# Pooled attention and a SoLU MLP on one core: x's lower half in two steps, the first product by banks, spreading matrices by ScalarE, a new order

## The chip, the core and the metric

The kernel runs on one core of one Trainium2 chip. The core has five engines that each work through their own instructions in order: TensorE (PE, matrix products), VectorE (DVE), ScalarE (ACT), GpSimd (POOL) and SyncE (SP), which here issues all DMAs. An engine that has to wait for another holds up everything that stands behind on its own line. TensorE works from SBUF into PSUM; PSUM's banks hold 512 float32 columns for 128 partitions each. The metric is device time in microseconds, the median of several executions.

## The reference, cut to what matters

```python
# q, k, v: (8 batches, 8 heads, 576 rows, 64)
k_p = k.reshape(B, H, Sp, pool, D).mean(axis=3)      # pool 8: 72 rows
v_p = v.reshape(B, H, Sp, pool, D).mean(axis=3)
scores = scale * np.matmul(q, k_p.transpose(0, 1, 3, 2))
attn = softmax(scores)                               # over 72
x = np.matmul(attn, v_p)                             # -> 4608 tokens x 512
h = x @ w_in                                         # 512 -> 1024
solu = h * softmax(h)                                # over 1024
ln = (solu - mean) / sqrt(var + 1e-6) * g_ln
out = ln @ w_out                                     # 1024 -> 512
```

q, k and v are float32; w_in, w_out and g_ln come as 64-bit floats, which the kernel reads as words and converts itself.

## The kernel before

**Precision.** Each number that goes into a product is split into an upper half in float16 and a lower half, the rest, also in float16. Each product is then three products of halves: upper with upper, upper with the weight's lower half, lower with upper.

**Tiles.** The 4608 tokens are 36 tiles of 128. Every pair of batches has nine: four tiles of the first batch, one mixed tile (64 tokens of each batch), four of the second. Tile 4 is the first mixed one.

**One tile's way.** Its queries are split (`q_hi`, `q_lo`) and transposed by a DMA (qT); TensorE makes the scores; VectorE takes their maximum, the difference, the sum and the division, ScalarE the exponential; the shares e are split (`e_hi` on ScalarE, `e_lo` on GpSimd) and transposed by a DMA (eT, L848). TensorE multiplies them with the pooled V (`av`, L865) into a PSUM tile hp of two banks, of which there are two. Out of hp ScalarE makes x's upper half (`x_hi`, L873) and VectorE the lower (`x_lo`, L879), both for all 512 columns (bank 0 holds the chunks c = 0, 1 of x, bank 1 the chunks 2, 3). The first product (`mm1`, L897, 24 matmuls) then writes hp over with the 1024 columns of h, 512 in each bank. VectorE takes the maximum (`h_max`, L907), ScalarE the exponential (`h_exp`), VectorE the product with it and its sum (`z_mul`, L942); ScalarE centres it and makes the upper half, GpSimd the lower (`z_lo`), each is transposed by a DMA (zT, L972), and TensorE makes the second product (`mm2`, L1029, 24 matmuls in one bank). ScalarE evicts it (`o_evac`, L1037) and a DMA stores it (L1047 for a mixed tile, L1050 for the others).

**The first product's order.** It has three parts of eight matmuls. EARLY is 1: for every tile but the first, parts 0 and 1 take the upper half of x, two of the four chunks each, with both halves of the weight; part 2 takes x's lower half. Within each the two banks take turns (`for f in range(2)`). The whole product waits for both halves of x.

**Pooled V.** GpSimd adds the rows of V in groups of 8 (L346, three halvings) and VectorE takes the largest of them (`amx_v`, L366). TensorE carries the maximum over the partitions (gv, L375), and from it VectorE makes a scale in four steps, the last into `sv` (L388 to L400). Part of the pooled V has then to lie in other partitions, which TensorE does by a product with matrices of zeros and ones: `pick`, filled by 24 casts of VectorE before anything else (L255), is read by `v_ex` (L482), and `v_put` (L488) writes the result, vbr, on VectorE.

**What sets the order.** The function records 2,255 operations in a list, each with an engine, what it reads and writes and a due time, and then calls them in the order of a table of numbers, ORDER. The order of the calls is each engine's order; the engines' waits for each other follow from the tiles that the calls read and write. A buffer of a pool that is asked for again waits for the readers of the one before.

Of the kernel before, what the change touches and what calls it, by code (L numbers as in the profile page):

```python
# [12 lines left out]
AF = mybir.ActivationFunctionType  # L13
# [5 lines left out]
S14 = float(2**14)  # L19
# [148 lines left out]
def kernel(  # L168
# [10 lines left out]
    nc = tc.nc  # L179
    B, H, S, D = q.shape  # L180
# [8 lines left out]
    R1 = SP - R0  # L189
# [1260 lines left out]
```

## Time and profile before

| | us |
|---|---|
| median of 3 runs | 491.08 (490.11 to 492.01) |
| profiled execution | 492.35 |
| its span | 490.6 |
| TensorE busy | 440.0 (90%) |
| VectorE busy | 358.8 (73%) |
| ScalarE busy | 351.5 (72%) |
| GpSimd busy | 322.0 (66%) |

The span is the time from the first to the last instruction that the profiler saw; the rest of the execution's time lies around it. A share of the whole span is a mean over stretches with different limits: in the first 60 us the weights are converted and the first tiles start, later the tiles follow each other at an even pace, so shares are to be read by stretch. The tables give a start in us from the span's start, a time in us, the engine, the line and the operation; "x16" are 16 instructions of one form in a row, and a bracket gives how long the engine had idled before and who ended it.

### The profile page before, as it was taken

The numbers are of one execution on the slowest core, as the hardware profiler recorded it, in microseconds if no ns is written. First come the engines' busy times: TensorE is split into PE (matmuls) and PEld (weight loads), VectorE is DVE, ScalarE is ACT, GpSimd is POOL, SyncE is SP. The second block draws the span as 40 slices with busy tenths as digits, with TensorE's granted clock in tenths as the row PEclk, the third lists the DMA queues.
The fourth block names the chain that finished last, engine by engine and source line by source line (L and its number), as shares of the span: only waits on it lengthen the run. The fifth ranks groups of instructions, "written<-read, shape, count | busy, mean of one in ns | idle before, by whom it ended". The sixth has DMA issues, their size and how long they took to land.

```text
span 490.6 us, 12671 instructions
## 1 busy us (share of the span) xinstructions
PE 440.0 (90%) x4890; PEld 213.3 (43%) x4890; DVE 358.8 (73%) x867; ACT 351.5 (72%) x584; POOL 322.0 (66%) x469
## 2 busy tenths in 40 slices
PE   0076779899997999999999999989999999999996
PEld 0033334354443444544444444444444544544463
DVE  6898999859876596778686876777668866847530
ACT  1796988868973679677878677758787877765671
POOL 4235499786886588794688768946679666453350
PEclk9998999999999899999999999999999999999999
DMA  8999896999799878999889987995996786752742
GB/s 287 353 231 293 199 171 138 210 202 178 192 197 215 178 122 182 218 183 175 229 195 205 209 139 180 208 190 125 202 215 163 185 164 126 133 125 53 154 108 64
DMA packets 198460, 89.51 MB, mean 182 GB/s; under 512 B 174208, under 2 KB 182656, under 8 KB 197888
## 3 DMA queue, kind: packets, MB, share of 16 engines
q1 hardware_dynamic: 198400, 88.70, 85.4%
q8 instruction: 38, 0.62, 0.5%
q14 instruction: 22, 0.18, 0.1%
HBM read 37.75 MB, written 9.44 MB: 96 GB/s over the span
## 4 chain that ended last, share of the span: by engine, by line
PE 49%; DMA 17%; POOL 12%; DVE 10%; ACT 6%; issue 3%; SPq 2%; POOLq 0%; DVEq 0%; ACTq 0%
PE op L1029 22%; PE hp L897 21%; DMA zT<-z 5%; DMA qr<-in_q_dram 5%; DMA vr<-in_v_dram 4%; POOL z L964 2%; PE hp L865 2%; PE sc L772 2%; DMA eT<-e 2%; POOL vr L346 2%; POOL kr L346 2%; DVE z L942 1%; ACT z L956 1%; POOL e L841 1%; DVE pick L255 1%
## 5 line engine op out<-in xcount | busy, mean ns | idle before, releaser
L1029 PE MATMUL op<-wo,zT 128*128 128x512 f16 (+1 forms) x888 | 199.5, 376 | 3.8 <-DMA zT<-z 2.9
L897 PE MATMUL hp<-wi,xT 128*128 128x512 f16 x864 | 195.2, 379 | 4.6 <-DVE xT L879 4.6
L897 PEld LDWEIGHTS <-xT 128*128 128x128 f16 x864 | 83.4, 98 | 103.5 <-issue 4.2
L1029 PEld LDWEIGHTS <-zT 128*128 128x128 f16 x888 | 84.2, 98 | 98.9 <-DMA zT<-z 5.7
L964 POOL TENSOR_TENSOR z<-z,z 128x512 f16<-128x512 f32 x71 | 82.3, 1170 | 53.8 <-ACT z L951 46.9
L907 DVE TENSOR_REDUCE m<-hp 128x1 f32<-128x1024 f32 x36 | 43.9, 1221 | 31.3 <-PE hp L897 31.1
L346 POOL TENSOR_TENSOR vr<-vr 128x256 f32<-128x256 f32 (+2 forms) x48 | 42.3, 883 | 23.8 <-DMA vr<-in_v_dram 23.1
L841 POOL TENSOR_TENSOR e<-e,e 128x512 f16<-128x512 f32 x36 | 42.0, 1168 | 20.6 <-ACT e L833 20.5
L956 ACT ACTIVATE z<-z,sz 128x1024 f16<-128x1024 f32 x36 | 41.2, 1145 | 19.6 <-DVE z L942 19.2
L942 DVE SCALAR_TENSOR_TENSOR z<-hp,rs,z 128x1024 f32<-128x1024 f32 x36 | 46.1, 1281 | 6.2 <-ACT z L918 4.9
L918 ACT ACTIVATE z<-hp,nb,Hb 128x1024 f32<-128x1024 f32 x32 | 38.3, 1198 | 14.1 <-DVE nb L910 13.5
L1037 ACT ACTIVATE osb<-op,f 128x512 f32<-128x512 f32 (+1 forms) x37 | 24.8, 669 | 30.4 <-issue 9.9
L346 POOL TENSOR_TENSOR kr<-kr 128x512 f32<-128x512 f32 (+3 forms) x48 | 40.8, 858 | 7.4 <-DMA kr<-in_k_dram 6.7
L951 ACT ACTIVATE z<-z,sz 128x1024 f32<-128x1024 f32 x36 | 41.2, 1145 | 0.9
L751 POOL TENSOR_TENSOR q<-qr,q 128x512 f16<-128x512 f32 x28 | 32.4, 1157 | 10.8 <-ACT q L741 10.7
L796 DVE TENSOR_REDUCE sc<-sc 128x8 f32<-128x576 f32 x36 | 27.4, 761 | 15.5 <-ACT sc L792 15.5
L977 ACT ACTIVATE junk<-z 128x1024 f16<-128x1024 f32 x36 | 37.7, 1048 | 0.3
L782 DVE TENSOR_REDUCE mx<-sc 128x8 f32<-128x576 f32 x36 | 27.0, 751 | 14.6 <-PE sc L772 13.6
L879 DVE SCALAR_TENSOR_TENSOR xT<-hp,xT 128x512 f16<-128x512 f32 x36 | 24.6, 683 | 14.0 <-ACT xT L873 13.7
L873 ACT ACTIVATE xT<-hp 128x512 f16<-128x512 f32 x36 | 21.3, 591 | 17.9 <-PE hp L865 17.8
L811 DVE TENSOR_TENSOR e<-sc,r 128x576 f32<-128x576 f32 x36 | 27.2, 756 | 2.2
L785 DVE TENSOR_TENSOR sc<-sc,mx 128x576 f32<-128x576 f32 x36 | 27.4, 762 | 0.8
(229 smaller groups left out, 584.3 us busy)
## 6 DMA issues: line engine op xcount, KB each, us to landing
qr<-in_q_dram SPq DMA_DIRECT2D x16, 512.0 KB, 5.2
kr<-in_k_dram SPq DMA_DIRECT2D x16, 512.0 KB, 5.0
out_dram<-osb SPq DMA_DIRECT2D x31, 256.0 KB, 3.0
wor<-in_moe_w_out_dram SPq DMA_DIRECT2D x4, 1024.0 KB, 11.3
vr<-in_v_dram SPq DMA_DIRECT2D x8, 512.0 KB, 4.5
vr<-in_v_dram SPq DMA_DIRECT2D x16, 256.0 KB, 6.0
wo<-in_moe_w_in_dram SPq DMA_DIRECT2D x2, 1024.0 KB
wir<-in_moe_w_in_dram SPq DMA_DIRECT2D x2, 1024.0 KB
```

The source lines that it names most:

```text
L346: nc.gpsimd.tensor_tensor(out=dst, in0=x[:, :, :n], in1=x[:, :, n : 2 * n], op=ALU.add)
L751: nc.gpsimd.tensor_tensor(out=q_dst(i, 1), in0=q_src(i), in1=q_dst(i, 0), op=ALU.subtract)
L841: nc.gpsimd.tensor_tensor(out=m[:, 1], in0=em, in1=m[:, 0], op=ALU.subtract)
L897: nc.tensor.matmul(hp[:, f], lhsT=xT[:, xt, 2 * (c % 2) + c // 2], rhs=wi[:, wt, c, f * 512 : (f + 1) * 512], start=(part == 0 and n == 0) ...
L907: nc.vector.tensor_reduce(out=small(i, "m"), in_=tl[i]["hp"], axis=AX.XY, op=ALU.max)
L918: nc.scalar.activation(z, t["hp"], AF.Exp, bias=t["nb"], scale=hsc(i, 0), accum_out=small(i, "se"))
L942: nc.vector.scalar_tensor_tensor(out=t["z"], in0=t["hp"], scalar=t["rs"], in1=t["z"], op0=ALU.mult, op1=ALU.mult, accum_out=small(i, "sz"),)
L951: nc.scalar.activation(t["zf"], t["zf"], AF.Identity, bias=t["sz"], scale=-float(DFF))
L956: nc.scalar.activation(t["z16"][:, 0], t["zf"], AF.Identity, bias=t["sz"], scale=-float(DFF))
L964: eng.tensor_tensor(out=t["z16"][:, 1, fs], in0=t["zf"][:, fs], in1=t["z16"][:, 0, fs], op=ALU.subtract)
L977: nc.scalar.activation(junk, t["zf"], AF.Square, scale=DFF**-0.5, accum_out=small(i, "V"))
L1029: nc.tensor.matmul(op_, lhsT=zT[:, zt, c], rhs=wo[:, wt, c, cols(hf)], start=(part == 0 and n == 0), stop=(part == 2 and n == len(todo) - 1),)
```

## The change

Four things. The 24 casts that fill `pick` are gone from VectorE; a new operation `spreader`, called four times, does it in four ScalarE copies each, and `v_ex` is recorded as a reader of `pick`. `x_lo` takes an index j and makes one bank's half (128x256). `mm1` goes by banks: part 0 all products of x's upper half into bank 0, part 1 those into bank 1, part 2 those of the lower half; part 0 is recorded behind the lower half's first step, part 1 behind its second. And ORDER is another table, 2,295 numbers, of which two lines stand for all.

```diff
 ORDER = (
-    3, 4, 177, 178, 12, 110, 0, 50, 2, 56, 179, 1, 180, 181, 51, 182, 183, 52, 185, 186, 231,
+    1, 3, 7, 181, 4, 54, 55, 8, 56, 2, 6, 60, 9, 10, 0, 182, 183, 184, 185, 186, 5, 11, 21, 25,
...
-    for j in range(2):
-        for n in range(HB):
-            c, g = divmod(n, 2)
-            unit = ident[:, 64 * j + 4 * c + 2 * j + g : 64 * j + 64 : H]
-            for x, s in ((0, 0), (1, 1), (0, 2)):
-                at = 64 * j + 32 * c + 8 * s
-                nc.vector.tensor_copy(out=pick[:, x, n, at : at + 8], in_=unit)
...
+    def spreader(n):
+        c, g = divmod(n, 2)
+        for x, ss in ((0, slice(0, 4, 2)), (1, slice(1, 2))):
+            for j in range(2):
+                to = pick[:, x, n, 64 * j + 32 * c : 64 * j + 32 * c + 32]
+                to = to.rearrange("p (s r) -> p s r", r=R1)[:, ss]
+                at = 64 * j + 4 * c + 2 * j + g
+                unit = ident[:, at : 64 * j + 64 : H]
+                nc.scalar.activation(to, unit.unsqueeze(1).to_broadcast(to.shape), AF.Copy)
...
-    def x_lo(i):
+    def x_lo(i, j):
         xT = tl[i]["xT"]
+        cs = slice(2 * j, 2 * j + 2)
         nc.vector.scalar_tensor_tensor(
-            out=xT[:, 1].rearrange("p (t c) m -> p t (c m)", t=2), in0=tl[i]["xp"],
-            scalar=1.0 / S14, in1=xT[:, 0].rearrange("p (t c) m -> p t (c m)", t=2),
+            out=xT[:, 1, cs].rearrange("p c m -> p (c m)"), in0=tl[i]["xp"][:, j],
+            scalar=1.0 / S14, in1=xT[:, 0, cs].rearrange("p c m -> p (c m)"),
             op0=ALU.mult, op1=ALU.subtract,
         )
...
             xt, wt = ((0, 0), (1, 0), (0, 1))[part]
-            todo = [(c, xt, wt) for c in range(CI)]
+            todo = [(f, c, xt, wt) for c in range(CI) for f in range(2)]
         elif part < 2:
-            todo = [(c, 0, wt) for c in (2 * part, 2 * part + 1) for wt in range(2)]
-        else:
-            todo = [(c, 1, 0) for c in range(CI)]
-        for n, (c, xt, wt) in enumerate(todo):
-            for f in range(2):
-                nc.tensor.matmul(
-                    hp[:, f], lhsT=xT[:, xt, 2 * (c % 2) + c // 2], rhs=wi[:, wt, c, f * 512 : (f + 1) * 512],
-                    start=(part == 0 and n == 0), stop=(part == 2 and n == len(todo) - 1),
-                )
+            todo = [(part, c, 0, wt) for c in range(CI) for wt in range(2)]
+        else:
+            todo = [(f, c, 1, 0) for c in range(CI) for f in range(2)]
+        for f, c, xt, wt in todo:
+            nc.tensor.matmul(
+                hp[:, f], lhsT=xT[:, xt, 2 * (c % 2) + c // 2],
+                rhs=wi[:, wt, c, f * 512 : (f + 1) * 512],
+                start=(c == 0 and xt == 0 and wt == 0), stop=(part == 2 and c == CI - 1),
+            )
...
-        op("pe", 0.28, t + 7.5, v_ex, b, r=[("vrt", b)], w=[("x", "v", b)])
+        op("pe", 0.28, t + 7.5, v_ex, b, r=[("vrt", b), ("pick",)], w=[("x", "v", b)])
...
-        op("dve", 0.69, t(-1, 8.2), x_lo, i, r=[("h", i)], w=K("xT1"), u=K("xT"), after=[n])
+        for j in range(2):
+            op("dve", 0.42, t(-1, 8.2 + 0.5 * j), x_lo, i, j, r=[("h", i)], w=[("xT1", i, j)],
+               u=K("xT"), after=[n])
...
-                ws = [(nm, "wi", d) for nm in ("whi", "wlo") for d in (2 * c, 2 * c + 1)]
+                ws = [(nm, "wi", d) for nm in ("whi", "wlo") for d in range(4)]
+                ws += [("xT1", i, c)]
             else:
-                ws = K("xT1")
-            prev = [op("pe", 1.727, t(0, 1.78 * c), mm1, i, c, r=K("xT", "xT1") + ws, w=[("h", i)],
+                ws = []
+            prev = [op("pe", 1.727, t(0, 1.78 * c), mm1, i, c, r=K("xT") + ws, w=[("h", i)],
                        after=prev if c else ready)]
```

**At the start, VectorE.** The first fence is VectorE's line before, from the maximum of the pooled V (`amx_v`) to the next tile's score maximum (mx); sc, r and e are softmax steps of tile 1, u_wo and wor the conversion of a chunk of w_out.

```order
L366 TENSOR_REDUCE amx_v<-vp_92 128x1
L796 TENSOR_REDUCE sc_369<-sc_369 128x2x4
L802 TENSOR_SCALAR sc_369<-sc_369 128x2x4
L806 RECIPROCAL r_445<-sc_369 128x8
L811 TENSOR_TENSOR e_447<-sc_369,r_445 128x576
L388 TENSOR_REDUCE pv_454<-gv_452 128x1
L393 TENSOR_SCALAR pv_454<-pv_454 128x1
L210 TENSOR_SCALAR pv_454<-pv_454 128x1
L400 RECIPROCAL sv_455<-pv_454 128x1
L533 TENSOR_SCALAR u_wo_437<-u_wo_437 128x1024
L554 SCALAR_TENSOR_TENSOR wor_354<-wor_354,u_wo_437 128x1024
L782 TENSOR_REDUCE mx_527<-sc_477 128x8
```

The same place in the new order:

```order
L362 TENSOR_REDUCE amx_v<-vp_92 128x1
L384 TENSOR_REDUCE pv_429<-gv_427 128x1
L389 TENSOR_SCALAR pv_429<-pv_429 128x1
L213 TENSOR_SCALAR pv_429<-pv_429 128x1
L396 RECIPROCAL sv_430<-pv_429 128x1
L802 TENSOR_REDUCE sc_360<-sc_360 128x2x4
L808 TENSOR_SCALAR sc_360<-sc_360 128x2x4
L539 TENSOR_SCALAR u_wo_438<-u_wo_438 128x1024
L812 RECIPROCAL r_446<-sc_360 128x8
L817 TENSOR_TENSOR e_452<-sc_360,r_446 128x576
L560 SCALAR_TENSOR_TENSOR wor_416<-wor_416,u_wo_438 128x1024
L788 TENSOR_REDUCE mx_513<-sc_464 128x8
```

The four steps to `sv` have moved from behind the softmax of tile 1 to directly behind `amx_v`.

**In tile 5, VectorE.** Before, x's lower half of tile 5 (xT5) stood between the maximum of tile 4's h (m4) and tile 7's score maximum (mx7); pz4, nb4 and rs4 are tile 4's small factors. Here the rows carry what each instruction waits for.

```order
L907 TENSOR_REDUCE m4_1576<-hp4_1453 128x1 [waits PE_49]
L910 TENSOR_SCALAR nb4_1579<-m4_1576,Hm0_1562 128x1 [waits DVE_49,Activation_49]
L879 SCALAR_TENSOR_TENSOR xT5_1619<-hp5_1586,xT5_1619 128x512 [waits Activation_49]
L782 TENSOR_REDUCE mx7_1673<-sc7_1624 128x8 [waits PE_49]
L925 TENSOR_SCALAR pz4_1675<-nb4_1579 128x1 [waits DVE_49]
```

In the new order, down to tile 4's `z_mul`:

```order
L914 TENSOR_REDUCE m4_1577<-hp4_1443 128x1 [waits PE_49]
L886 SCALAR_TENSOR_TENSOR xT5_1612<-hp5_1579,xT5_1612 128x256 [waits Activation_49]
L917 TENSOR_SCALAR nb4_1666<-m4_1577,Hm0_1515 128x1 [waits DVE_49]
L932 TENSOR_SCALAR pz4_1668<-nb4_1666 128x1 [waits DVE_49]
L937 TENSOR_SCALAR pz4_1668<-pz4_1668 128x1 [waits DVE_49]
L788 TENSOR_REDUCE mx7_1693<-sc7_1616 128x8 [waits PE_49]
L941 RECIPROCAL pz4_1668<-pz4_1668 128x1 [waits DVE_49]
L886 SCALAR_TENSOR_TENSOR xT5_1612<-hp5_1579,xT5_1612 128x256 [waits PE_49]
L943 TENSOR_SCALAR rs4_1699<-pz4_1668,Hm0_1515 128x1 [waits DVE_49]
L791 TENSOR_TENSOR sc7_1616<-sc7_1616,mx7_1693 128x2x288
L949 SCALAR_TENSOR_TENSOR z4_1670,sz4_1702<-hp4_1443,rs4_1699,z4_1670 128x1024 [waits DVE_49,Activation_49]
```

The one step on xT5 has become two with six others between them; the second half waits for TensorE, the first, like the whole before, for ScalarE.

**Ahead of tile 9's eT, SyncE.** Before, from the transpose qT10 to the transpose eT9; osb4 is the output of the mixed tile 4, zT7 the transposes of tile 7's z.

```order
L758 DMA_TRANSPOSE qT10_2226<-q16_10_2026 128x8x128
L301 DMA vr3_1_2231<-in_v_dram 64x2x512 x2
L758 DMA_TRANSPOSE qT11_2236<-q16_11_2087 128x8x128
L972 DMA_TRANSPOSE zT7_2249<-z16_7_2247 128x8x128
L1047 DMA out_0_dram<-osb4_2075 64x512 x2
L972 DMA_TRANSPOSE zT7_2249<-z16_7_2247 128x8x128
L307 DMA vr3_2_2317<-in_v_dram 64x1x512 x2
L1050 DMA out_0_dram<-osb6_2245 128x512
L316 DMA qr3_2410<-in_q_dram 128x4x256
L848 DMA_TRANSPOSE eT9_2428<-e16_1_101 128x10x128
```

In the new order, from the store of osb4 on:

```order
L1054 DMA out_0_dram<-osb4_2070 64x512 x2
L764 DMA_TRANSPOSE qT10_2160<-q16_10_2157 128x8x128
L764 DMA_TRANSPOSE qT11_2223<-q16_11_2037 128x8x128
L303 DMA vr3_2_2277<-in_v_dram 64x1x512 x2
L1057 DMA out_0_dram<-osb5_2311 128x512
L979 DMA_TRANSPOSE zT7_2408<-z16_7_2289 128x8x128 x2
L854 DMA_TRANSPOSE eT9_2469<-e16_1_101 128x10x128
L1057 DMA out_0_dram<-osb6_2155 128x512
```

The store of osb4 has moved from between the two transposes of z to ahead of qT10, and eT9 stands directly behind both of them, with the store of osb5 before them.

## Rows read from the trace of the kernel before

**Rows 1.** Busy us by stretch: PE, PEld, DVE, ACT, POOL; then clock, DMA, GB/s.

```profile
7.40:13.00 5.60, 0.37 (x2) 0.10 (x1) 5.60 (x26) 0.01 (x1) 4.31 (x5) 1.00 1.04 392
49.90:61.00 11.10, 9.31 (x118) 4.49 (x118) 10.97 (x25) 10.29 (x22) 5.16 (x9) 1.00 0.85 182
...
160.20:163.60 3.40, 3.40 (x31) 1.31 (x22) 2.14 (x4) 1.31 (x3) 0.19 (x1) 0.50 1.18 147
...
163.70:486.90 323.20, 317.85 (x3487) 155.78 (x3485) 225.40 (x552) 234.31 (x393) 215.00 (x315) 1.00 0.81 165
```

**Rows 2.** PE's waits (us, times, longest), 98 to 491; last line: 49 to 98.

```profile
PE hp L865 <- DMA eT<-e: 3.5, 3, 2.6
...
PE sc L772 <- DVE pq('b', 6)_5636 L393: 0.3, 1, 0.3
...
PE hp L897 <- DVE xT L879: 4.6, 3, 1.8
```

**Rows 3.** The chain of waits: start, us, what.

```profile
7.48 5.50 DVE pick L255 x24
...
23.76 11.65 DMA vr<-in_v_dram
...
37.69 0.46 POOL vp L346
...
49.90 3.61 PE hp L897 x16
...
54.02 1.85 PE hp L897 x8
...
55.90 1.23 DVE m L907
```

**Rows 4.** Duration by line: ns min/median/max, first and last start, forms.

```profile
L835 ACT ACTIVATE e<-e x72: 238/242/258, 33.5 to 452.3; 128x64 f16<-128x64 f32 x72
...
L879 DVE SCALAR_TENSOR_TENSOR xT<-hp,xT x36: 639/681/692, 49.2 to 461.6; 128x512 f16<-128x512 f32 x36
...
L746 DVE SCALAR_TENSOR_TENSOR q<-qr,sq('b', 0)_174,q x8: 472/500/1265, 14.7 to 37.0; 128x256 f16<-128x256 f32 x8
...
L897 PE MATMUL hp<-wi,xT x864: 376/379/390, 49.9 to 467.4; 128*128 128x512 f16 x173
```

**Rows 5.** VectorE's instructions in order of time, 39 to 50 us.

```profile
39.27 0.49 DVE L366 TENSOR_REDUCE amx_v<-vp 128x1 bf16<-128x320 f32 x1 [1.29 <-POOL vp L346]
39.67 0.76 DVE L796 TENSOR_REDUCE sc<-sc 128x8 f32<-128x576 f32 x1
...
41.59 0.28 DVE L388 TENSOR_REDUCE pv<-gv 128x1 f32<-128x128 f32 x1
...
42.36 0.68 DVE L533 TENSOR_SCALAR u_wo<-u_wo 128x1024 int32<-128x1024 int32 x1
...
45.05 0.74 DVE L782 TENSOR_REDUCE mx<-sc 128x8 f32<-128x576 f32 x1
...
47.17 0.42 DVE L488 CAST vbr<-vx 128x256 f16<-128x256 f32 x1 [0.78 <-PE vx L482]
...
48.11 0.76 DVE L785 TENSOR_TENSOR sc<-sc,mx 128x576 f32<-128x576 f32 x1
...
49.16 0.68 DVE L879 SCALAR_TENSOR_TENSOR xT<-hp,xT 128x512 f16<-128x512 f32 x1
```

**Rows 6.** TensorE's instructions in order of time, 150 to 164 us.

```profile
153.13 3.62 PE L1029 MATMUL op<-wo,zT 128*128 128x512 f16 x16
159.36 0.36 PE L865 MATMUL hp<-eT,vb 64*64 64x128 f16 x12 [2.61 <-DMA eT<-e]
...
160.41 3.48 PE L1029 MATMUL op<-wo,zT 128*128 128x512 f16 x8
```

**Rows 7.** SyncE's DMAs in order of time, 147 to 156 us.

```profile
147.45 1.22 SPq L1047 DMA_DIRECT2D out_dram<-osb  x2
```

**Rows 8.** ScalarE's instructions in order of time, 147 to 156 us.

```profile
151.58 0.69 ACT L1037 ACTIVATE osb<-op,f 128x512 f32<-128x512 f32 x1 [3.75 <-DMA out_dram<-osb]
```

More of the change, by code (lines that the diff above doesn't have):

```diff
@@ L1243 @@
     home_free = []
+    for n in range(HB):
+        op("act", 0.85, 0.5 + n, spreader, n, w=[("pick",)])
     loads_kv(0, "kr", 0.0, 0.01)
@@ L1332, in tile @@
                 ws = (
-                    [("whi", "wi", d) for d in range(4)], K("xT1"),
+                    [("whi", "wi", d) for d in range(4)] + [("xT1", i, j) for j in range(2)], [],
                     [("wlo", "wi", d) for d in range(4)],
```

277 rows, old and new, of the table ORDER are left out of this document.

## The prediction

> **What bounds the kernel now.** I read the busy times by stretch first. From 163.7 us to the end of the products TensorE is busy 317.85 of 323.20 us [rows 1]; VectorE works 225.40 of them, ScalarE 234.31, GpSimd 215.00. There a change pays only in what TensorE waits for or loses. Before that others set the pace: in 49.9 to 61.0 us VectorE is busy 10.97 of 11.10 us and TensorE 9.31. Next, who TensorE waits for after 98 us [rows 2]: five rows from 3.5 us (the transpose eT, one wait of it 2.6) down to 0.3, 3.5 + 1.9 + 1.7 + 0.7 + 0.3 = 8.1 us. Last the chain of waits at the start [rows 3]: 5.50 us of the 24 casts that write `pick`, then 11.65 us of V's load, and the first product starts only at 49.90 us.
>
> **The casts leave VectorE.** 5.5 us go from VectorE's line; the 16 small ScalarE copies that replace them are like the 128x64 copy of 0.242 us [rows 4], so 3.9 us. ScalarE is busy 0.01 of 5.60 us where the casts stood [rows 1], which hides them; if they stuck out, only the matmuls with `pick` near 47 us would wait for them, so zero. But the 5.5 us don't come out of the first product's start. What follows on the chain is V's load, and its DMAs stand on SyncE behind the same loads and the same two transposes as before, so I leave its landing at 35.41 us (23.76 + 11.65). GpSimd's three additions behind it end near 38.2 in the new order (the third starts at 37.69 and takes 0.46 [rows 3], with no e work between now), against `amx_v` at 39.27 before [rows 5]. In the new order the four steps that give `sv` follow on `amx_v` directly, without tile 1's softmax (39.67 to 41.59 before). So `sv` is there at 38.2 + 0.5 + 0.3 (a matmul and two hand-overs, 0.22, 0.03 and 0.06 as below) + 0.8 (41.59 to 42.36) = 39.8, not 42.4: 2.6 earlier. Behind it now stand, ahead of `vbr`: softmax 1.9, shift and tail of w_out 2.7 (42.36 to 45.05), the maximum 0.7 and the difference 0.8 = 6.1, so `vbr` at 45.9 to 46.0, not 47.17. From there to the lower half of x 2.0 us before, 2.2 now (the quarter maximum of q comes behind `vbr`), and two halves take 0.16 longer than the whole. The first product moves from 49.90 to about 49.1: -0.8. Bounds: +0.5, if V's load lands later by the load of g that now stands in front of its second part, and -5.5, if the whole of the casts came off the front.
>
> **x's lower half in two steps.** One whole takes 681 ns [rows 4]. A half isn't in the trace. From 512 to 1024 columns out of PSUM VectorE's time grows to 1.23 us (the maximum [rows 3]), by 0.55, which takes a half to 0.41 us; the nearest 256-column one, out of SBUF, took at least 472 ns. I take 0.42, between them: 0.16 us more per tile, 5.8 us for 36. Where TensorE is the bound VectorE has nearly 100 us free [rows 1]; in 49.9 to 61.0 it has 0.13, and two tiles fall there: +0.3. The Trainium skill speaks against such halves: its page "VectorE: DVE Perf Modes", section on the errata with a fixed latency per instruction, gives (120 + columns) cycles at 0.96 GHz out of PSUM and advises 512 or more elements, so 0.66 and 0.39 us. The whole took 0.68 here; no run shows the half. By the page the total above is 4.5 us and the two tiles' share 0.25.
>
> **The first product bank by bank.** The number of matmuls stays, and eight in a row into one bank are no slower: L1029 does that already, 16 in 3.62 us [rows 6], so one each 0.216 us. What should be gained is the wait of the product for the whole lower half (three of them in 49 to 98 us, 4.6 us [rows 2]). The order with its waits shows otherwise. Where both halves stand ahead of the product's first part, that part waits for the later half. In 14 of 36 tiles (2, 3, 4, 5, 7, 14, 17, 18, 19, 21, 22, 23, 32, 33) the second half is written behind the first part, and then VectorE has to wait for that part's eighth matmul, although it reads the other bank; then the second part waits for the half. In tiles 3, 14 and 23 other matmuls stand between the parts; in 11 none do. So in each of these TensorE stands still: a matmul lasts 0.379 us [rows 4] and the next could go after 0.216, so 0.163 to drain; 0.03 to VectorE (the eighth ended at 54.02 + 1.85 = 55.87, the maximum started at 55.90 [rows 3]); 0.42 for the half; 0.06 back (49.16 + 0.68 = 49.84 to 49.90 [rows 3, 5]): 0.67 us. Tiles 2 and 4 lie ahead of 98 us, where TensorE has waits anyway. Nine by 0.67 = +6.0. Bounds: 0, if these tiles' TensorE would have waited for something later all the same, and 11 by 0.73 = +8.0. Behind the waiting half on VectorE's line stand other tiles' softmax and z steps (in tile 5 `rs4` and tile 4's product z), held for up to 1.73 us, eight matmuls.
>
> The Trainium skill, "PSUM — Partial Sum Buffer", section on bank collisions, says to guard PSUM by bank and quadrant: an engine may read one bank while another writes the next. By that rule the wait isn't needed, the half would lie beside the first part, and the six microseconds would be away: 485.2 in place of 491.2. No run here shows it; the waits that the program holds are by tile.
>
> **The new order.** The largest single loss after 98 us is at tile 9 [rows 6]: TensorE idles 2.61 us before 159.36 and then eight matmuls take 3.48 us and not 1.73 (8 by 0.216), since the granted clock stands at 1.2 GHz, 0.50 of its full 2.4 [rows 1]: 2.61 + 1.75 = 4.4 us. Its cause is the store of tile 4's output: issued at 147.45 behind a transpose z, so ScalarE waited 3.75 us to evict the next output, and tile 9's exponentials, queued behind that, came late [rows 7, 8]. In the new order that store stands ahead of qT10. I take the 4.4 as gone; bound 0, if the stop stays. The other 5.5 us of rows 2: between the end of a tile's first product and the start of its second, 73 product matmuls stand now in the mean, 64 before (counted over the whole order), so the z transposes have 2 us more; the distance from scores to the e product hasn't grown. I take -1.0, with bounds of -5.5 (all gone) and +4.4 (one new stop like tile 9's).
>
> **Sum.** -0.8 + 0.3 + 6.0 - 4.4 - 1.0 = +0.1. The profiled execution took 492.35 us, its span 490.6; that is 1.27 above the median of 491.08. So 492.45, and against the median 491.2.
>
> **Rivals.** *The order wins* (0.30): the second halves' waits lie beside waits that were there anyway or the reserve takes the remaining 4.5 us of waits, and V lands 1.2 earlier: 491.2 - 4.5 - 1.2 = 485.5. For it speaks the greater reserve; against it that nothing in the trace lets V land earlier, and that a wait of 0.67 us inside a product has nothing to lie beside. *The stop at tile 9 stays* (0.30): eT9 stands on SyncE now behind both halves of zT7, the second of which needs GpSimd, and behind the store of tile 5; if one of them comes as late as tile 4's store did, the 4.4 us are lost again: 495.6. It decides from 3 us: with more than half of the 4.4 left the result is slower. VectorE's held line speaks for it, the store's new place against. *The product doesn't start by banks* is no rival but the forecast.
>
> **How the numbers follow.** Forecast 491.2, chance 0.40, its own range 487.5 to 494.5. A measurement of this kernel tells 0.5%, 2.46 us, from no change, so faster is under 488.6 and slower over 493.5. Of the forecast's 0.40 I lay 0.06 on faster, 0.31 on same, 0.03 on slower. With the rivals: faster 0.36, same 0.31, slower 0.33. The range, 484.0 to 497.0, takes in both rivals and leaves out the ends at which all bounds of one sign meet.
>
> **What would show it.** Right: gaps of about 0.5 us on TensorE in the middle of the first product of tiles 5, 7, 17, 18, 19, 21, 22, 32 and 33, ended by VectorE's x step; none in tiles 8 to 13; the first product at 49 us and V's load still on the chain; no half clock near 160 us. Wrong: the first product at 46 us or earlier (then V's load wasn't the limit), no gaps inside the products, or a stop for eT of over 2 us in the new order.

## The result, and the profile after

The changed kernel took 496.38 us (median of 4 runs, 495.72 to 498.11) against 490.6 us of the kernel before beside it: ratio 1.0123, 95% interval 1.0083 to 1.0162. In a later round it was 495.81 against 491.26: 1.0079 (1.0048 to 1.0111). It is slower, by 5.8 us the first time and by 4.6 the second. The forecast was 491.2, no change; the time lies in its range, 484 to 497, but near the upper end, where a rival stood. The profiled execution took 496.07 us, its span 494.3, 3.7 more than the span before.

The busy times by stretch (columns as in [rows 1]) of the changed kernel:

```profile
49.90:61.00 11.10, 9.13 (x109) 3.97 (x108) 9.43 (x23) 6.87 (x16) 6.92 (x10) 0.81 0.88 247
163.70:490.60 326.90, 318.24 (x3485) 155.64 (x3484) 227.61 (x580) 230.72 (x392) 213.11 (x311) 1.00 0.79 165
```

TensorE does the same work, but in the long stretch 8.7 us of its time are idle, where they were 5.4 in [rows 1]; in the early one its mean clock is 0.81 and not 1.00. Who TensorE waits for from 98 us on (us, times, longest), to be read against [rows 2]:

```profile
PE hp L903 <- DVE xT L886: 8.7, 13, 1.6
PE sc L778 <- DVE pq('b', 5)_4635 L213: 1.2, 1, 1.2
PE hp L871 <- DMA eT<-e: 0.9, 1, 0.9
PE op L1036 <- DMA zT<-z: 0.9, 1, 0.9
PE hp L903 <- DVE pv L213: 0.5, 1, 0.5
```

The waits for transposes of [rows 2] have shrunk to 1.8 us. In their place stands one row that wasn't there after 98 us: the first product waits for VectorE's step on x, 13 times. (The 0.5 us put down to `pv` are a fourteenth: the wait in tile 17, of the same length and at the same place.)

What such a wait looks like is seen in tile 5. TensorE's line, then VectorE's, in order of time:

```profile
114.00 1.89 PE L903 MATMUL hp<-wi,xT 128*128 128x512 f16 x8
116.40 1.89 PE L903 MATMUL hp<-wi,xT 128*128 128x512 f16 x8 [0.52 <-DVE xT L886]
```

```profile
113.53 0.41 DVE L886 SCALAR_TENSOR_TENSOR xT<-hp,xT 128x256 f16<-128x256 f32 x1
...
115.09 0.15 DVE L941 RECIPROCAL pz<-pz 128x1 f32<-128x1 f32 x1
115.92 0.42 DVE L886 SCALAR_TENSOR_TENSOR xT<-hp,xT 128x256 f16<-128x256 f32 x1 [0.69 <-PE hp L903]
116.26 0.21 DVE L943 TENSOR_SCALAR rs<-pz,Hm 128x1 f32<-128x1 f32 x1
...
117.05 1.28 DVE L949 SCALAR_TENSOR_TENSOR z<-hp,rs,z 128x1024 f32<-128x1024 f32 x1
```

The first eight matmuls end at 115.89; only then VectorE may start the second half (115.92), which ends at 116.34; TensorE goes on at 116.40. VectorE had stood still for 0.69 us in front of it, with tile 4's `rs` and product z behind. In tile 19 it stood far longer, and somebody else paid for that. VectorE, then TensorE:

```profile
279.39 0.42 DVE L886 SCALAR_TENSOR_TENSOR xT<-hp,xT 128x256 f16<-128x256 f32 x1
282.73 0.42 DVE L886 SCALAR_TENSOR_TENSOR xT<-hp,xT 128x256 f16<-128x256 f32 x1 [2.92 <-PE hp L903]
...
286.07 0.14 DVE L213 TENSOR_SCALAR pq('b', 5)_4635<-pq('b', 5)_4635 128x1 int32<-128x1 int32 x1
```

```profile
280.80 1.89 PE L903 MATMUL hp<-wi,xT 128*128 128x512 f16 x8
283.20 1.89 PE L903 MATMUL hp<-wi,xT 128*128 128x512 f16 x8 [0.52 <-DVE xT L886]
286.30 0.58 PE L778 MATMUL sc<-kT,qT 64*64 64x72 f16 x48 [1.21 <-DVE pq('b', 5)_4635 L213]
```

TensorE stops for 0.52 us inside the product, and 3 us later for another 1.21, since the scale of batch 5's queries stands behind the held steps on VectorE's line. All halves together (columns as in [rows 4]; below, us and times that VectorE waited, and that TensorE waited for it):

```profile
L886 DVE SCALAR_TENSOR_TENSOR xT<-hp,xT x72: 405/416/426, 46.9 to 464.0; 128x256 f16<-128x256 f32 x72
...
  PE hp L903: 17.1, 11
...
  PE hp L903: 12.3, 16
```

VectorE stood still 17.1 us in eleven waits for TensorE, each of them for the first part of a product. Tile 9, where before the largest stop was [rows 6]: TensorE, SyncE, VectorE.

```profile
159.31 0.36 PE L871 MATMUL hp<-eT,vb 64*64 64x128 f16 x12
...
163.84 4.48 PE L903 MATMUL hp<-wi,xT 128*128 128x512 f16 x20 [1.58 <-DVE xT L886]
```

```profile
143.77 1.27 SPq L1054 DMA_DIRECT2D out_dram<-osb  x2
...
154.00 1.36 SPq L854 DMA_TRANSPOSE eT<-e  x1
```

```profile
160.64 0.43 DVE L886 SCALAR_TENSOR_TENSOR xT<-hp,xT 128x256 f16<-128x256 f32 x1
162.24 1.22 DVE L362 TENSOR_REDUCE amx_q<-qr 128x1 bf16<-128x1024 f32 x1 [1.18 <-DMA qr<-in_q_dram]
163.38 0.41 DVE L886 SCALAR_TENSOR_TENSOR xT<-hp,xT 128x256 f16<-128x256 f32 x1
```

The mixed tile's store goes out 3.7 us earlier than in [rows 7], eT9 comes in time, no wait stands ahead of 159.31, and the granted clock stays at 1.00 (the first 20 matmuls of the product in 4.48 us). But the product of tile 9 then waits 1.58 us at its start: its second half stands on VectorE's line behind a maximum that waits for a load of q.

### The profile page after: what moved, and what is told of

Read it like the earlier page. It is cut to its first block, busy times and chain, and to the rows that moved or that the text cites. A ratio compares the mean times of both kernels' runs of the same rounds, so it can differ in the third digit from the quotient of the medians.

```text
span 494.3 us, 12702 instructions
## 1 busy us (share of the span) xinstructions
PE 440.6 (89%) x4890; PEld 213.0 (43%) x4890; DVE 355.0 (72%) x879; ACT 351.5 (71%) x600; POOL 322.1 (65%) x469
## 4 chain that ended last, share of the span: by engine, by line
PE 61%; DVE 11%; DMA 5%; ACT 3%; POOL 3%; issue 2%; SPq 1%; ACTq 0%; POOLq 0%; DVEq 0%
PE hp L903 28%; PE op L1036 27%; PE hp L871 2%; DMA eT<-e 2%; PE sc L778 2%; DVE xT L886 2%; DVE m L914 2%; DVE wo L692 1%; DVE z L949 1%; POOL z L971 1%; DMA qr<-in_q_dram 1%; DMA zT<-z 1%; DMA out_dram<-osb 1%; DVE sc L791 1%; DVE sc L802 1%
## 5 line engine op out<-in xcount | busy, mean ns | idle before, releaser
L903 PE MATMUL hp<-wi,xT 128*128 128x512 f16 x864 | 199.5, 384 | 13.0 <-DVE xT L886 12.3
L1036 PE MATMUL op<-wo,zT 128*128 128x512 f16 (+1 forms) x888 | 196.5, 374 | 2.4 <-DMA zT<-z 0.9
L886 DVE SCALAR_TENSOR_TENSOR xT<-hp,xT 128x256 f16<-128x256 f32 x72 | 29.3, 418 | 25.9 <-PE hp L903 17.1
L839 ACT ACTIVATE e<-e 128x512 f16<-128x512 f32 x36 | 22.3, 618 | 9.4 <-DVE e L817 8.1
```

Source lines behind the costliest of these rows:

```text
L886: nc.vector.scalar_tensor_tensor(out=xT[:, 1, cs].rearrange("p c m -> p (c m)"), in0=tl[i]["xp"][:, j], scalar=1.0 / S14, in1=xT[:, 0, cs] ...
L903: nc.tensor.matmul(hp[:, f], lhsT=xT[:, xt, 2 * (c % 2) + c // 2], rhs=wi[:, wt, c, f * 512 : (f + 1) * 512], start=(c == 0 and xt == 0 an ...
L1036: nc.tensor.matmul(op_, lhsT=zT[:, zt, c], rhs=wo[:, wt, c, cols(hf)], start=(part == 0 and n == 0), stop=(part == 2 and n == len(todo) - 1),)
```

## The experiments

All numbers are medians of the kernel and ratios to the kernel before on the same chip, with 95% intervals. "T" is the theory that the place of the second halves costs the time. The changed kernel's 496.38 us come from another round than the experiments: the kernel before took 490.6 us beside it, and 492.1, 492.01 and 491.26 us in the three rounds of experiments, each on another chip. Where medians of two rounds are subtracted below, the difference is uncertain by 1 to 2 us.

**The halves together.** In every tile the second half is recorded directly behind the first:

```diff
+            order.remove(halves_of[i, 1])
+            order.insert(order.index(halves_of[i, 0]) + 1, halves_of[i, 1])
```

> The changed kernel with one edit: in every tile the second half of x's lower half is recorded directly behind the first, ahead of the first product; nothing else moves. Theory T (the second half's place): in the changed kernel's trace eleven tiles (2, 4, 5, 7, 17, 18, 19, 21, 22, 32, 33) lose 0.68 us each in the middle of the product, since VectorE waits for its first part, and four (9, 15, 30, 35) wait 1.58 + 1.18 + 0.95 + 0.37 = 4.1 us at its start for a second half that stands late on VectorE's line. With the halves together ten tiles after 98 us give back 6.8, the four 4.1; in tiles 5, 18 and 33, where the first half ended only 0.05, 0.18 and 0.15 us ahead of the product, 0.9 comes back as a wait at the start. So -10.0: about 486.4 against 496.4. Rival R (the waits lie there because TensorE has to wait for something anyway): TensorE then waits for the transposes of z and e or for scales instead, and no more than 3 us is gained: 493.4 or more.

Measured: 483.21 us, 0.9829 (0.979 to 0.9868). Thirteen us come back (13.2 between the medians; 14.7 if each is taken by its distance from the kernel before beside it), and the kernel is faster than before. TensorE's waits from 98 us on, all of them:

```profile
PE sc L778 <- DMA qT<-q: 0.4, 1, 0.4
PE hp L903 <- DVE xT L886: 0.3, 1, 0.3
```

Nothing took the place of the waits removed, so rival R falls; the gain is 3 us more than T's sum.

**Eleven tiles, four tiles.** The same edit for two groups of tiles: those with the stop inside the product, and those with a wait at its start.

> The changed kernel with the second half directly behind the first in tiles 2, 4, 5, 7, 17, 18, 19, 21, 22, 32 and 33 alone, those whose product stood still in the middle. T: ten by 0.68 less 0.9 at the start of tiles 5, 18 and 33: -5.9, 490.5. R: under 2 us gained, 494.5 or more.

> The changed kernel with the second half directly behind the first in tiles 9, 15, 30 and 35 alone, whose product waited at its start. T: -4.1, 492.3; this and the eleven tiles together make what the edit of all tiles makes. R: under 1.5 us, since what stood ahead of those halves on VectorE (another tile's z step or softmax) is late by 0.42 instead: 495 or more.

Measured: 485.4, 0.9866 (0.9822 to 0.991), and 491.48, 1.0009 (0.9975 to 1.0044): 11.0 and 4.9 us less than the changed kernel. The four tiles give what was expected within the scatter of single runs (490.0 to 494.8); the profiled executions are only 1.8 us apart in span, and TensorE waits 5.3 us for x's lower half where it waited 8.7. The eleven give 5 more than the stops themselves. Part of that is seen in the traces. The waits for batch 5's scale (1.2 us) and for eT (0.9) of the changed kernel are absent where the eleven tiles are mended:

```profile
PE hp L903 <- DVE xT L886: 4.7, 4, 2.2
PE op L1036 <- DMA zT<-z: 0.7, 1, 0.7
PE hp L903 <- DVE pq('b', 7)_6775 L213: 0.2, 1, 0.2
```

and are still there where only the four are (1.2 and 0.7 us). So the held VectorE costs about two of the five us. The profiled executions differ by 8.7 us in span, and of these the stops (6.8) and the two waits (2.1), less 0.6 us that the four other tiles wait longer (4.7 against 4.1), make 8.3. From 8.7 to 11.0 it is only the distance of these two executions from their medians: the one with the eleven tiles was the longest of its six (487.39 us, the median 485.4). The two groups together come to 15.9, the edit of all tiles to 13.2; with runs that spread over 3 to 5 us that is no contradiction, and no proof of a sum either.

**One whole step.** x's lower half in one step of 512 columns at the place of the first half:

```diff
-        cs = slice(2 * j, 2 * j + 2)
+        if j:
+            return
         nc.vector.scalar_tensor_tensor(
-            out=xT[:, 1, cs].rearrange("p c m -> p (c m)"), in0=tl[i]["xp"][:, j],
...
+            out=xT[:, 1].rearrange("p (t c) m -> p t (c m)", t=2), in0=tl[i]["xp"],
...
```

> The changed kernel with x's lower half again made in one step of 512 columns, at the place of the first half; the product by banks, the copies on ScalarE and the order stay. T: as with the halves together, and a little less, since one step is 0.16 us shorter than two and the product waits less at the start of tiles 5, 18 and 33 (0.3 us in all): 485 to 487. R: 493 or more. If the halves as such were what costs (5.4 us more of VectorE in all), this one would be clearly under the halves together, by 2 us or more.

Measured: 483.28, 0.9829 (0.9789 to 0.987), the same as with the halves together, and 2 us under the range of T. That x comes in halves costs nothing that can be measured; where the second one stands does.

**Ten other tiles.** The halves together, but with the second half behind the product's first part again in ten tiles that had no such wait:

```diff
+            late = i in (8, 10, 12, 16, 24, 25, 28, 29, 31, 34)
+            at = first_part[i] if late else halves_of[i, 0]
-            order.insert(order.index(halves_of[i, 0]) + 1, halves_of[i, 1])
+            order.insert(order.index(at) + 1, halves_of[i, 1])
```

> The kernel with the halves together (483.21) with the second half put behind the product's first part again, but in ten other tiles (8, 10, 12, 16, 24, 25, 28, 29, 31, 34), in which the changed kernel had no such wait. T: ten stops of 0.52 us idle and 0.16 drained, 6.8 us, and up to 4 us more through what VectorE holds up behind the waiting half (with the eleven tiles 11.0 us came back for 6.8 of stops): 490 to 494. Rival: the loss belonged to what surrounds those eleven tiles, and TensorE has the time here: under 486.

Measured: 501.01, 1.0201 (1.0169 to 1.0234): 17.8 us more than with the halves together, so the loss goes with the place, not with the eleven tiles. It is 7 us above the range of T. In tile 8 one sees why; VectorE, then TensorE:

```profile
149.02 0.76 DVE L788 TENSOR_REDUCE mx<-sc 128x8 f32<-128x576 f32 x1 [1.20 <-PE sc L778]
...
152.74 0.76 DVE L817 TENSOR_TENSOR e<-sc,r 128x576 f32<-128x576 f32 x1
153.42 0.41 DVE L886 SCALAR_TENSOR_TENSOR xT<-hp,xT 128x256 f16<-128x256 f32 x1
```

```profile
148.72 1.90 PE L903 MATMUL hp<-wi,xT 128*128 128x512 f16 x8
153.88 3.04 PE L903 MATMUL hp<-wi,xT 128*128 128x512 f16 x8 [3.27 <-DVE xT L886]
```

The half stands there behind a whole softmax on VectorE's line, whose first step waits 1.20 us for scores itself, so the stop is 3.27 us, and the next eight matmuls take 3.04 and not 1.89: the granted clock fell too, to 0.60 in the mean of these 3.04 us. Six of the ten stops are the 0.52 us of T; the others are 3.27 (tile 8), 2.41 (tile 28), 2.06 (25) and 1.31 (10). The ten come to 12.1 us, their drains to 1.6, and the lower clock behind tiles 8 and 28 to about 3.3 (tile 28's last sixteen matmuls, for one, took 5.27 and not 3.61 us), which is 17.0 of the 17.8 us. So 0.68 us is the smallest price of such a stop, not its mean.

**The order alone.** Casts on VectorE, one whole step, the product with the banks in turn: the kernel before with nothing but the new order (of the edits the one in the product is shown).

```diff
...
-            todo = [(part, c, 0, wt) for c in range(CI) for wt in range(2)]
...
+            todo = [(c, 0, wt) for c in (2 * part, 2 * part + 1) for wt in range(2)]
...
```

> The kernel before with the new order alone: the 24 casts are back on VectorE, x's lower half is one step (at the place of the first half), the product has the order of before (banks in turn). Theory O (the order carries the gain that the kernel with one whole step showed against the kernel before, 483.3 against 492.1): 483 to 486, with 1 to 2 us lost at the start to the casts. Rival B (the product by banks or the copies carry it): 488 or more.

> The new order alone once more, on the same chip as the other three: 479 to 483.

Measured: 481.05, 0.9758 (0.9715 to 0.98), and again 480.89, 0.9779 (0.9751 to 0.9807). It is the fastest version of all, 11.0 and 10.4 us under the kernel before and 2 us under the range of theory O. TensorE's waits from 98 us on, in the first of the two:

```profile
PE op L1037 <- DMA zT<-z: 0.7, 1, 0.7
PE hp L905 <- DVE xT L887: 0.2, 1, 0.2
```

Busy times from 98 to 420 us (columns as in [rows 1]), before and then with the new order alone:

```profile
98.00:420.00 322.00, 313.28 (x3668) 152.14 (x3670) 238.16 (x582) 238.93 (x408) 238.41 (x347) 0.99 0.91 183
```

```profile
98.00:420.00 322.00, 321.07 (x3797) 156.91 (x3796) 247.99 (x602) 243.77 (x420) 242.61 (x352) 1.00 0.90 187
```

TensorE has 0.9 us of 322 left to lose, before it had 8.7.

**The other parts alone, and with the order.** The casts as ScalarE copies in the old order; halves and banks in the old order (both halves in one operation); the new order with the copies, but without halves and banks.

```diff
...
-                nc.vector.tensor_copy(out=pick[:, x, n, at : at + 8], in_=unit)
...
+                nc.scalar.activation(to, unit.unsqueeze(1).to_broadcast(to.shape), AF.Copy)
```

> The kernel before with one edit: the 24 casts on VectorE are 16 copies on ScalarE, at the same place; everything else is before's. In the changed kernel the first product came 2.15 us earlier than before, and 3.3 us were given back by 98 us, two thirds of it at a half clock (16 matmuls in 5.30 us and not 3.61, eight in 3.35 and not 1.89). If the casts bound the start, the first product comes 2 to 5 us earlier and 1 to 4 us are left in the total, less what the clock takes: 488 to 491 against 492. If V's load binds it, nothing: 491 to 493.

> The kernel before with x's lower half in two steps, one right behind the other, and the product by banks; the casts and the order are before's. The halves as such cost VectorE 0.155 us more for a tile (two of 0.418 against 0.681), so where the product waits for them, in the tiles that waited before (0, 1, 2, 34), 0.6 us; the banks nothing. 0 to +1: 491 to 493 against 492. If halves or banks as such are dear (as the changed kernel's total would have it by itself), 495 or more.

> The new order with x's lower half in one step and the product as before, but with the copies on ScalarE (the new order alone, with the casts on VectorE, took 481.05). If the copies gain in this order what they gained in the old one (0.5%), 478.6; if the start is hidden behind what VectorE and ScalarE have to do until 98 us, 480 to 483; if the product by banks is what made the kernel with one whole step 2.2 us slower than the new order alone, 481; if the copies did, 483.

Measured: copies in the old order 490.05, 0.9949 (0.9919 to 0.9979); halves and banks in the old order 491.89, 0.9995 (0.9964 to 1.0026); order and copies 482.71, 0.9824 (0.9795 to 0.9852). Halves and banks are worth nothing by themselves, and the copies, not the product by banks, make the kernel with one whole step slower than the new order alone. The copies gain 2.0 us in the old order and lose 1.8 in the new one (482.71 against 480.89 on the same chip, runs 482.1 to 484.7 against 478.9 to 481.7). The profiled executions show where. TensorE at the start, with the order and the copies, then with the order alone on that chip:

```profile
46.31 0.36 PE L871 MATMUL hp<-eT,vb 64*64 64x128 f16 x12 [1.89 <-ACT wi L690]
...
48.44 6.27 PE L905 MATMUL hp<-wi,xT 128*128 128x512 f16 x16 [0.99 <-DVE xT L887]
```

```profile
47.64 3.61 PE L905 MATMUL hp<-wi,xT 128*128 128x512 f16 x16 [0.98 <-DVE xT L887]
```

With the copies the first product starts 0.8 us later, not earlier. TensorE waits for the evictions of w_in's lower half (L690), which stand on ScalarE's line behind a step (L527) that waits 1.93 us for a load of w_out; with the casts that step waits for nothing. And the product runs at a granted clock of 0.57 in place of 1.00. These two executions are 3.9 us apart in span, and 3.3 of them are there by the maximum of tile 4's h. From there to the end they gain nearly the same on the kernel before, 10.7 us with the copies and 11.3 without. How much of the 1.8 us is the later start and how much the clock isn't separated.

**TensorE kept busy at the start.** The kernel with one whole step, and 21 matmuls into a PSUM tile that nobody reads, where TensorE waits ahead of the first two products:

```diff
...
+        for _ in range(n):
+            nc.tensor.matmul(
+                fills[0], lhsT=pick[:, 0, 0], rhs=pick[:, 0].rearrange("p n m -> p (n m)"), start=True, stop=True
+            )
```

> The kernel with one whole step in the new order, and on TensorE 21 matmuls more (128x512, into a PSUM tile that nobody reads) where it waits at the start: 5 ahead of tile 0's e product, 4 ahead of the maximum of the mixed queries, 4 and 8 ahead of the first products of tiles 0 and 1. Theory C (the half clock behind those waits costs up to 3.5 us, in some executions more than in others; the runs without the fill spread from 480.9 to 485.0): the runs come together near the lower end, 479 to 481.5. Rival: until 98 us VectorE and ScalarE set the pace and the clock costs nothing in the total, or the added matmuls delay what they stand before: 483 or more.

Measured: 484.44, 0.9832 (0.9787 to 0.9877), against 483.28 without; runs from 483.5 to 486.7. The clock did what was wanted:

```profile
47.38 1.03 PE L865 MATMUL fill<-pick 128*128 128x512 f16 x4
48.53 3.61 PE L920 MATMUL hp<-wi,xT 128*128 128x512 f16 x16
...
57.07 1.89 PE L920 MATMUL hp<-wi,xT 128*128 128x512 f16 x8
```

but the total didn't. Theory C, that the half clock at the start is what the total loses, falls in this form. That the clock costs nothing there isn't shown by it: the first product started later with the fill (48.53 us against 47.75), TensorE waited 2.2 us from 98 us on against 0.7, and the execution of the kernel without it that was profiled, its shortest, ran the first sixteen matmuls in 3.61 us as well. So the rival's delay and the clock stay mixed.

**The changed kernel again**, unedited, beside the last of these:

> The changed kernel once more, unedited, on the same chip as the other three: 495 to 498; with the runs of before on this chip the ratio is 1.008 to 1.013.

Measured: 495.81, 1.0079 (1.0048 to 1.0111), just under the lower end of the expected ratio.

## Why the prediction was right and wrong

The mechanisms were the right ones; two large terms of opposite sign were each taken at half their size, and the remainder had the wrong size with it: +0.1 forecast, +5.8 measured. The pieces measured apart make +4.0: -11.0 for the order alone, +1.8 for the copies in it, +13.2 for the place of the second halves.

That the time lies in the range of 484.0 to 497.0 is in part luck. It lies outside the forecast's own range, 487.5 to 494.5. The upper end was there for the rival that the stop at tile 9 stays, 495.6; that stop went away, and other waits brought the time to the same place.

**The second halves: +6.0 forecast, about +13 measured.** The stop was right in every piece: 0.52 us idle and 0.16 drained, 0.68 against 0.67. So was the list: tiles 5, 7, 17, 18, 19, 21, 22, 32 and 33, and tiles 2 and 4 as well; tile 4's stop fell at 107 us, behind the bound of 98, so ten counted and not nine. What failed is what the prediction named and then priced at nothing. It wrote that the product waits for the later half where both stand ahead of it: four tiles with the halves far apart on VectorE's line lost 4.1 us in that way (4.9 in the experiment). And it wrote that other tiles' steps are held behind the waiting half, for up to 1.73 us: VectorE stood 17.1 us in eleven waits (tile 23's among them, tile 33's not), 2.5 to 2.9 us in tiles 4, 19 and 32, where it had come to the half long before the product began; scores and an e product waited 2.1 us that are gone where the eleven tiles are mended. Ten stops at 0.68 are 6.8, with 4.1 and 2.1 that is 13.0. The bound of +8.0 was no bound, since it counted only the stop.

**The new order: -5.4 forecast (-4.4 and -1.0), -11 measured.** The stop at tile 9 went away for the reason given, and the half clock with it. The other 5.5 us of waits, of which 1.0 was taken as gained, went as well: the order alone has 0.9 us of waits left after 98 us. The end of -5.5 in the bounds was the nearest value. The sum can be rebuilt, as an estimate: 8.3 us of waits in before (those of [rows 2] and one of 0.2), 1.75 of half clock and 0.16 drained at each of eleven waits (1.8) are 11.9, less the 0.9 left, 11.0. In the two traces of the order alone, 10.9 and 11.3 us lie behind the maximum of tile 4's h. So "the order wins" was right of the order, and the halves that stood in it took it back.

**The first product: -0.8 forecast, -2.16 in the trace.** VectorE and TensorE of the changed kernel at the start:

```profile
36.18 0.49 DVE L362 TENSOR_REDUCE amx_v<-vp 128x1 bf16<-128x320 f32 x1 [0.34 <-POOL vp L342]
...
42.73 0.41 DVE L494 CAST vbr<-vx 128x256 f16<-128x256 f32 x1
```

```profile
44.86 0.36 PE L871 MATMUL hp<-eT,vb 64*64 64x128 f16 x12 [1.25 <-ACT wi L690]
...
47.74 5.30 PE L903 MATMUL hp<-wi,xT 128*128 128x512 f16 x16 [1.04 <-DVE xT L886]
...
58.16 3.35 PE L903 MATMUL hp<-wi,xT 128*128 128x512 f16 x8 [1.97 <-DVE xT L886]
```

`amx_v` came at 36.2, not 38.2 as the sum had it; V's landing was not as fixed as the prediction took it: GpSimd began to add V's last part at 33.21 us, before at 35.54. With `vbr` at 42.7 the next late one is ScalarE's eviction of w_in's lower half (L690). It doesn't matter in the end: at the first product of tile 4 the changed kernel was 1.13 us behind before (104.68 against 103.55), and the copies alone, which brought the first product 3.0 us forward in the old order, left 2.0 us in the total. Nor do the casts' 5.5 us show in the new order: with the casts still on VectorE the first product started at 47.72 and 47.64 us, as early as in the changed kernel (47.74, and 48.16 in the later round). There it is the order that moved it. That others than TensorE set the first 98 us fits this; the experiment with the filled waits doesn't show it.

**The small terms.** A half takes 0.416 us, where 0.42 was taken. By the errata section of the Trainium skill's page "VectorE: DVE Perf Modes" it would be 0.39, an estimate; the trace sides with the higher one. The 16 copies lay in time that ScalarE had idle, 0.206 us each, but they were not free, as the new order with them shows:

```profile
L480 ACT ACTIVATE pick<-ident x16: 197/206/229, 2.8 to 4.5; 128x16 f16<-128x16 f32 x8, 128x8 f16<-128x8 f32 x8
```

Of the signs named ahead, the gaps inside the products and the full clock near 160 us were right; the first product at 49 us and V's load on the chain were not. What is open: how the 1.8 us that the copies cost in the new order divide between the later start and the clock. Whether the second half could run beside the first part on the other bank wasn't tried, since the waits of this program go by tile.

## What to carry to other kernels

Before a step is cut in two so that its consumer can start earlier, look where the second piece stands in its engine's line and what it waits for: here a stop of 0.52 us inside a product became one of 3.27 where a softmax stood between the pieces, and what was queued behind the waiting piece cost more. Price an order by the sum of all waits that it can remove where one engine is at 97%, not by the largest, and test it apart from the edits that came with it: the new order alone was worth 11 us, and what it came with, above all the place of the second halves in it, took more than that away. A wait that a prediction mentions needs a number, even a rough one.

## What the runs showed of the hardware

The granted clock at the start differed between kernels that ran the same matmuls there. The first sixteen of tile 0 took 3.61 us at 2.4 GHz in both traces of the new order alone, after waits of 1.55 and 0.98 us, and in the kernel with one whole step, after 1.05 us. They took 5.30, 6.27 and 6.50 us, partly or mostly at 1.2 GHz (a mean granted clock of 0.68, 0.57 and 0.55), in the changed kernel, in the order with the copies and in the halves together, after waits of 1.04, 0.99 and 1.12 us. The length of the last wait does not tell which it will be, and 21 filling matmuls kept the clock up without a gain in the total. Within one kernel the executions at the higher clock were the shorter ones: with the eleven tiles mended, three at a mean granted clock of 1.00 took 483.4 to 484.1 us, and three at 0.986 to 0.993 took 486.8 to 487.4.
